# Mapping the memory's keys in the projections' layout, turning them by transposing transfers, and making a segment's sums in the next segment's query stage

## The chip, the cores and the metric

The kernel runs on one core of one Trainium2 chip. The metric is the device time of one execution in microseconds (us). A core has a matrix engine (TensorE, PE in the profile; PEld is its weight load), a vector engine (VectorE, DVE), a scalar engine (ScalarE, ACT), a general engine (GpSimd, POOL) and a queue engine that issues nearly all transfers here (SyncE, SP). Each engine works through its own instructions in the order in which they were written, and waits on semaphores for the others.

## The reference

Two independent results stand side by side in the output: an attention with a compressive memory on `A_x`, and a Fourier mixing layer on `B_x`. The change touches only the memory of the first. With 2048 rows, width 576, 32 heads of 18, cut into four segments of 512 rows:

```python
phi = lambda t: jnp.where(t > 0, t + 1.0, jnp.exp(t))
for s in range(N):
    qs, ks, vs = q[:, :, s], k[:, :, s], v[:, :, s]
    logits = jnp.einsum("bhqd,bhkd->bhqk", qs, ks) * scale + mask
    p = _softmax(logits, axis=-1)
    a_dot = jnp.einsum("bhqk,bhkd->bhqd", p, vs)
    pq = phi(qs)
    num = jnp.einsum("bhld,bhde->bhle", pq, M)
    den = jnp.einsum("bhld,bhd->bhl", pq, z)[..., None] + 1e-6
    o = g * (num / den) + (1.0 - g) * a_dot
    outs.append(o)
    pk = phi(ks)
    M = M + jnp.einsum("bhld,bhle->bhde", pk, vs)
    z = z + jnp.einsum("bhld->bhd", pk)
```

The sums M and z of a segment contract over its 512 rows, so the matrix engine needs the mapped keys `pk` with rows on the partitions.

## The kernel before

**Stages.** The first stage (to about 215 us) makes, for each of the four segments, the query and key projections and then the value projection, looks into the memory, and sums the mapped keys times the values into the memory. Float32 numbers are cut into a high and a low float16 part throughout, so a product is three matrix products. Beside this, the first stage loads and cuts the Fourier input and weights. The second stage (the rest, over three quarters of the time) interleaves the softmax attention of 32 head groups with the dense products of the Fourier layer; its order is set by a table of places and a head start of `LOW["head"]` dense steps.

**A segment in the first stage.** `open_qk(s)` writes products for the first four of nine column blocks m (0 to 3 queries, 4 to 7 keys, 8 the last 64 columns of both): first the terms of input parts k = 0 and 1 for all four blocks, then the rest. Then, for m in (0, 1, 2, 3, 8, 4, 5, 6, 7), `project_qk` makes the remaining products, ACT copies each block out (a key block stays as a float32 tile `KF[m]`, columns on the partitions, rows along it), DVE takes its largest value, POOL makes a scale from that, and for s > 0 a query block is mapped by `phi` for the memory. Then, for four row tiles j, `project_v` makes two half products of 288 columns each, ACT and DVE cut them (tiles `vs`, `vn`, `vr`), and the generator `lookup` reads the memory for s > 0.

**Mapped keys before.** In `project_v`, after the first half of tile j, `k_natural(j)` turns the five key blocks' 128 rows with five float32 PE transposes into two PSUM tiles `kt`; ACT makes relu from each (320 and 256 columns) and exp over all 576, DVE adds them (line 482, twice), casts to float16 (line 483, `knh`), and POOL or DVE subtracts for the low part (line 484, `knl`). This is done for 12 tiles: three segments of four. `kn` and `vn` have two buffers, by j. `accumulate(j)` (line 664) multiplies mapped keys with `vn[j]` into three PSUM tiles in 11 products; it stands after `project_v(j + 1)`, and that of the last tile, j = 3, inside the next segment's `open_qk`. `memory()` then reads the sums out (ACT line 673, DVE line 675), masks them on POOL, and cuts them four ticks later.

**The order.** Cuts of keys, queries, Fourier input and hidden weights are placed by the table `TIMES` in slots (13 a segment: nine projections, four row tiles); `timed(n)` writes all that is due by slot n. `ENGINES` says for each low part whether DVE (0) or POOL (1) makes it. `later(1, ...)` puts a call, mostly a transfer, into the next tick. The cut tiles `p` (two float16 parts of 512) share five buffers; each is held until its transfers have landed.

Of the kernel before, what the change touches and what calls it, by code (L numbers as in the profile page):

```python
# [12 lines left out]
F32 = mybir.dt.float32  # L13
# [11 lines left out]
P = 128  # L25
# [205 lines left out]
def infini_attention_and_fnet(ctx: ExitStack, tc: tile.TileContext, xT, wqk, w8, wv, wo, beta, xbT, cT, hT, out):  # L231
# [270 lines left out]
    def open_qk(s):  # L502
# [5 lines left out]
        for a, b in zip(edges, edges[1:]):  # L508
            for m in ms:
                for n in range(a, b):  # L510
                    pe.matmul(FIRST[m], *terms[m][n], start=n == 0, stop=n == 13)  # L511
# [88 lines left out]
    def k_natural(j):  # L600
        js = slice(j * P, (j + 1) * P)
        e = sk.tile([P, D], F32, name="ke", bufs=2)
        sources = []
        for ms in ((8, 4, 5), (6, 7)):
            o = ps.tile([P, L], F32, name="kt", tag="acc", bufs=5)
            for n, m in enumerate(ms):
                pe.transpose(o[:, n * P:(n + 1) * P], KF[m][:, js], ident)
            sources.append((e[:, :320], o[:, 64:384]) if ms[0] == 8 else (e[:, 320:], o[:, :256]))
        phi("keys", e, sources, *kn[j % 2])

    def project_v(s, j, meanwhile):
# [4 lines left out]
        for h in range(2):  # L616
# [10 lines left out]
            if s < 3:  # L627
                cut16(vn[j % 2][:, 0, hs, :DH], vn[j % 2][:, 1, hs, :DH], o)
            dve.tensor_tensor(r[:, hs], o, vs[:, hs, 18:36], OP.subtract)
            if h == 0 and s < 3:  # L630
                k_natural(j)
# [17 lines left out]
    def accumulate(j, which=(0, 1)):  # L649
        (kh, kl), v = kn[j % 2], vn[j % 2]  # L650
        for n in which:
            for c in range(5):
                b, at, both = SUMS[c]
                o = sums(c)
                fs = slice(64 + c * P, 64 + (c + 1) * P) if c < 4 else slice(0, 64)
# [7 lines left out]
                for keys, values, to in todo:  # L663
                    pe.matmul(to, keys[:, fs], values, start=b not in started, stop=True, skip_group_check=True)
                    started.add(b)
# [169 lines left out]
    def value_load(G):  # L835
        if G < NG:
# [6 lines left out]
            2.64, 2.86, 6.22, 7.98, 10.74, 10.75, 14.61, 15.81, 19.93, 18.76, 22.19, 22.72, 25.41, 26.05, 28.15,  # L843
            29.07, 33.85, 32.47, 38.83, 42.49],
        "fourier_high": [
            3.24, 5.15, 9.1, 9.18, 12.67, 12.17, 17.74, 17.24, 21.8, 19.26, 24.11, 24.59, 27.01, 27.83, 30.08, 30.44,
            35.63, 35.31, 41.59, 43.21],
        "fourier_low": [
            5.87, 7.07, 9.69, 9.65, 12.88, 15.09, 18.71, 18.31, 21.84, 20.05, 24.3, 25.26, 27.11, 28.68, 31.96, 31.13,
            37.93, 35.46, 41.63, 43.55],  # L850
        "key_high": [
            8.87, 11.85, 12.5, 11.11, 5.49, 19.93, 19.02, 22.3, 26.42, 21.45, 34.62, 35.55, 42.28, 37.46, 32.06,
            45.61, 46.36, 50.73, 48.45, 43.61],
        "key_low": [
            11.93, 12.19, 14.6, 11.93, 6.4, 19.97, 26.66, 23.27, 29.12, 21.93, 35.99, 38.96, 45.01, 38.19, 33.18,
            46.24, 47.23, 51.28, 51.81, 44.15],
        "query_high": [
            7.81, 6.66, 12.61, 11.74, 19.01, 25.83, 25.22, 25.79, 34.42, 38.56, 38.99, 36.6, 46.88, 47.84, 49.98, 48.0],
        "query_low": [
            10.08, 9.16, 13.03, 11.77, 19.53, 25.89, 25.95, 26.64, 34.54, 38.66, 39.13, 38.71, 49.92, 47.94, 50.19,  # L860
            48.47],
        "x_load": [
            8.68, 8.9, 9.11, 9.96, 10.88, 14.1, 16.66, 16.93, 18.62, 21.07, 29.06, 29.2, 32.1, 34.28, 36.66],
        "x_split": [
            11.44, 11.98, 18.79, 21.04, 34.56, 36.26],
        "hidden_high": [
            44.5, 44.99, 45.26, 46.07, 47.52],
        "hidden_low": [
            45.92, 45.29, 45.66, 50.24, 50.14]}
# [850 lines left out]
```

## Time and profile before

| | us |
|---|---|
| median of 3 runs | 932.0 (930.23 to 934.66) |
| the profiled execution | 932.74 |
| its span on the core | 931.2 |
| end of the first stage's last product on PE | about 215.5 |

PE was busy for 905.1 us of the span, DVE 743.0, ACT 694.9, POOL 560.1. These shares are means over two unlike stages. In the profile, a row of the view of groups gives line, engine, operation, tile written and tiles read, shapes, the count, busy time and mean length of one, and the idle time just before them with its releaser. A row of the view of waits says who waited for whom: us in total, how often, the longest. A row of the table of stretches gives, for a stretch of time, the busy us of PE, PEld, DVE, ACT and POOL with their instruction counts, then the granted PE clock as a share of full speed, the share of the transfer engines, and GB/s. The change lies wholly in the first stage, so its waits and stretches are what is to be read.

### The profile page before, as it was taken

How to read it: one execution, taken by the hardware profiler on the slowest of the kernel's cores; microseconds unless marked ns; L12 is line 12 of the kernel's file. 1: busy time of each engine (PE TensorE's matmuls, PEld its weight loads, DVE VectorE, ACT ScalarE, POOL GpSimd, SP SyncE). 2: the span in 40 equal slices, each digit the busy share in tenths (PEclk: the TensorE clock that was granted, in tenths of full speed). 3: DMA queues.
4: the chain of work that ended last, by engine and by line, in shares of the span. 5: the costliest groups of instructions: out<-in, count | busy, mean ns of one | idle time of the engine just before them, and what ended most of it. 6: DMA issues, size and time to landing. Idle time of an engine off the chain costs nothing.

```text
span 931.2 us, 25620 instructions
## 1 busy us (share of the span) xinstructions
PE 905.1 (97%) x9250; PEld 658.6 (71%) x9250; DVE 743.0 (80%) x2125; ACT 694.9 (75%) x1687; POOL 560.1 (60%) x843
## 2 busy tenths in 40 slices
PE   9999999998999999999999999999999999999997
PEld 5644746566677777777777777777777677777996
DVE  7878989978967768887788878887888888785784
ACT  6676768774767778888778877888789777885442
POOL 2334546544444557756786677668656896677560
PEclk9999999999999999999999999999999999999999
DMA  8466565769665437876888788887988897975552
GB/s 254 145 221 200 185 219 190 248 207 298 172 138 144 126 97 188 190 207 190 205 203 216 183 192 213 197 211 184 215 216 217 184 217 188 211 171 155 164 175 93
DMA packets 283128, 177.67 MB, mean 191 GB/s; under 512 B 204881, under 2 KB 240977, under 8 KB 282961
## 3 DMA queue, kind: packets, MB, share of 16 engines
q1 hardware_dynamic: 282768, 175.82, 70.9%
q8 instruction: 74, 1.21, 0.6%
q14 instruction: 62, 0.50, 0.2%
q10 hardware_dynamic: 224, 0.14, 0.1%
HBM read 90.00 MB, written 44.83 MB: 145 GB/s over the span
## 4 chain that ended last, share of the span: by engine, by line
PE 61%; ACT 12%; DVE 11%; DMA 5%; POOL 4%; issue 4%; SPq 1%; ACTq 0%; DVEq 0%; POOLq 0%
PE d L965 29%; PE pv L1497 4%; PE d L1009 3%; PE d L1011 3%; PE d L1010 3%; PE s L1365 3%; PE t L1251 3%; PE v L281 2%; PE pv L1498 2%; DVE s L1373 2%; ACT pd L1461 2%; PE s L1251 2%; PE d L1251 2%; ACT pf L1399 1%; PE d L1016 1%
## 5 line engine op out<-in xcount | busy, mean ns | idle before, releaser
L965 PEld LDWEIGHTS <-cs 128*128 128x128 f16 x3072 | 293.3, 98 | 84.8 <-issue 13.6
L965 PE MATMUL d<-wide,cs 128*128 128x288 f16 x2592 | 337.2, 286 | 0.0
L1373 DVE CUSTOM_DVE_ANT_0 s<-s,causal 128x384 f32<-128x384 f32 (+2 forms) x320 | 147.4, 498 | 62.6 <-PE s L1365 22.3
L1477 POOL TENSOR_TENSOR plo<-pd,phi 128x384 f16<-128x384 f32 (+1 forms) x116 | 120.0, 1054 | 3.3 <-ACT phi L1470 3.2
L1399 ACT ACTIVATE pf<-s,nb 128x384 f32<-128x384 f32 (+3 forms) x256 | 117.4, 526 | 5.0 <-DVE negm L1373 1.8
L329 POOL TENSOR_TENSOR cs<-craw,cs 128x512 f16<-128x512 f32 x88 | 103.5, 1178 | 28.9 <-ACT cs L795 26.4
L1412 POOL TENSOR_TENSOR hl<-pf,hl 128x512 f16<-128x512 f32 x50 | 58.5, 1176 | 98.4 <-ACT hl L1407 87.2
L1412 DVE TENSOR_TENSOR hl<-pf,hl 128x512 f16<-128x512 f32 (+1 forms) x142 | 94.4, 689 | 12.9 <-ACT hl L1407 12.5
L1373 DVE CUSTOM_DVE_ANT_0 t<-t,causal 128x384 f32<-128x384 f32 (+1 forms) x192 | 98.5, 541 | 2.2
L1407 ACT ACTIVATE hl<-pf 128x512 f16<-128x512 f32 (+1 forms) x192 | 93.2, 553 | 2.4 <-DMA ptt<-hl 2.4
L795 ACT ACTIVATE cs<-craw 128x512 f16<-128x512 f32 x128 | 80.4, 628 | 3.4 <-PE d L965 3.4
L1465 POOL TENSOR_SCALAR_AFFINE_SELECT pd<-pd 128x512 f32<-128x512 f32 x64 | 45.2, 706 | 61.0 <-ACT pd L1461 61.0
L1395 ACT ACTIVATE nb<-nb 128x2 f32<-128x2 f32 (+1 forms) x96 | 19.8, 206 | 72.8 <-DVE nb L1373 72.7
L1457 ACT ACTIVATE phi<-t 128x384 f16<-128x384 f32 x128 | 63.7, 497 | 6.7 <-PE t L1450 3.5
L965 PE MATMUL d<-ab,cs 128*128 128x288 f16 x480 | 66.6, 288 | 0.0
L281 PE MATMUL v<-wide,xh 128*128 128x288 f16 x256 | 49.5, 291 | 1.4 <-DVE w L717 0.6
L1365 PEld LDWEIGHTS <-st 54*128 54x128 f16 x512 | 19.6, 94 | 41.0 <-issue 35.1
L1365 PE MATMUL s<-st 54*128 54x256 f16 (+3 forms) x320 | 43.0, 296 | 5.4 <-ACT pf L1399 3.0
L511 PE MATMUL qk<-xh,wide 128*128 128x512 f16 x128 | 43.0, 391 | 0.6 <-ACT xh L251 0.4
L511 PEld LDWEIGHTS <-wide 128*128 128x128 f16 x224 | 21.4, 100 | 28.8 <-issue 4.9
L1019 ACT ACTIVATE wide<-d 128x288 f16<-128x288 f32 x54 | 22.2, 416 | 24.7 <-PE d L1016 24.1
L281 PE MATMUL qk<-xh,wide 128*128 128x512 f16 x128 | 40.7, 379 | 0.0
(346 smaller groups left out, 2319.6 us busy)
## 6 DMA issues: line engine op xcount, KB each, us to landing
craw<-cT SPq DMA_DIRECT2D x128, 256.0 KB
vd<-vs SPq DMA_DIRECT2D x16, 440.0 KB
vst<-vd SPq DMA_DIRECT2D x32, 220.0 KB
st<-qd SPq DMA_DIRECT2D x64, 108.0 KB
st<-kd SPq DMA_DIRECT2D x64, 108.0 KB
wide<-xbT SPq DMA_DIRECT2D x20, 256.0 KB
xk<-xd SPq DMA_DIRECT2D x20, 256.0 KB
out<-y SPq DMA_DIRECT2D x16, 288.0 KB
```

Of the source, the lines that this page charges most:

```text
L281: pe.matmul(o, a, b, start=n == 0, stop=n == len(terms) - 1)
L329: fn(*a)
L511: pe.matmul(FIRST[m], *terms[m][n], start=n == 0, stop=n == 13)
L795: act.activation(t[:, 0], raw, AF.Copy)
L965: pe.matmul(o[h], a, b[:, h * 288:h * 288 + 288], start=start, stop=stop)
L1251: pe.matmul(o, a, b, start=first and i == 0, stop=True, skip_group_check=True)
L1365: pe.matmul(o[half][:, first + c:first + c + w], q[r, x, i * P:w], k[r, x, :w], start=True, stop=True)
L1373: dve.tensor_tensor_reduce(x, x, CAUSAL[0][:, L - w:], scale=scale, scalar=-LOWEST, op0=OP.add, op1=OP.min, accum_out=into[:, 4 * half + i ...
L1399: act.activation(f[kind][half][:, to:to + w], o[half][:, c:c + w], AF.Exp, bias=nb[:, 4 * half + i:4 * half + i + 1], scale=-1.0)
L1407: act.activation(hl[half][:, 0, F_COL[kind]:F_COL[kind + 1]], f[kind][half], AF.Copy)
L1412: engine.tensor_tensor(hl[half][:, 1, a:b], f[kind][half], hl[half][:, 0, a:b], OP.subtract)
L1477: engine.tensor_tensor(lo[:, a:b], f, hi[:, a:b], OP.subtract)
```

## The change

Each key block is mapped where it lies, columns on the partitions, by the new `key_features(n)`: relu from `KF`, exp, one DVE add and one DVE cast over 512 rows, and the low part. There are 15 of these, three segments of five blocks; the last block of a segment has 64 partitions and a tile of its own, `k8`, the other four take a `p` tile. One transposing transfer per block then writes both parts, eight squares of 128 by 128, into `kn[c]`. The 60 PE transposes and their `kt` tiles go. `vn` gets four buffers, `kn` one for each block. All four `accumulate` calls of a segment move to the next segment's query stage: two behind the second projection and two behind the third, with `memory()` behind them. `TIMES` gets a row for the 15 features and new numbers elsewhere, `ENGINES` new choices, `LOW["head"]` goes from 3 to 2.

```diff
-    kn = []
+    kn = [sk.tile([P, 8, P], F16, name=f"kn{c}") for c in range(5)]
+    k8 = sk.tile([P, 2, L], F16, name="k8")
+    pool.memset(k8[:64], 0.0)
...
-    for i in range(2):
-        kn.append(tuple(sk.tile([P, D], F16, name=f"kn{n}{i}") for n in "hl"))
+    for i in range(4):
...
-                if s and m == 0 and a:
-                    accumulate(3, (1,))
-            if s and a == 0:
-                accumulate(3, (0,))
...
-    def k_natural(j):
-        js = slice(j * P, (j + 1) * P)
-        e = sk.tile([P, D], F32, name="ke", bufs=2)
-        sources = []
-        for ms in ((8, 4, 5), (6, 7)):
-            o = ps.tile([P, L], F32, name="kt", tag="acc", bufs=5)
-            for n, m in enumerate(ms):
-                pe.transpose(o[:, n * P:(n + 1) * P], KF[m][:, js], ident)
-            sources.append((e[:, :320], o[:, 64:384]) if ms[0] == 8 else (e[:, 320:], o[:, :256]))
-        phi("keys", e, sources, *kn[j % 2])
+    def key_features(n):
+        s, c = divmod(n, 5)
+        rows = slice(0, P) if c < 4 else slice(64, P)
+        e = sk.tile([P, L], F32, name="ke", bufs=2)[rows]
+        t = sb.tile([P, 2, L], F16, name="p", tag="p", bufs=5) if c < 4 else k8
+        phi("keys", e, ((e, KF[c + 4][rows]),), t[rows, 0], t[rows, 1])
+        later(1, nc.sync.dma_start_transpose, kn[c], t.rearrange("p a t -> p (a t)"))
...
-            if h == 0 and s < 3:
-                k_natural(j)
...
-        (kh, kl), v = kn[j % 2], vn[j % 2]
+        v = vn[j]
...
-                fs = slice(64 + c * P, 64 + (c + 1) * P) if c < 4 else slice(0, 64)
+                kh, kl = (kn[c][:, j + i, 64 * (c // 4):] for i in (0, 4))
...
         "x_split": [
-            11.44, 11.98, 18.79, 21.04, 34.56, 36.26],
+            10.72, 10.49, 18.71, 17.16, 35.42, 34.9],
...
+        "keys": [
+            11.53, 7.47, 10.5, 12.1, 6.81, 22.03, 20.47, 24.9, 24.5, 20.2, 33.58, 34.3, 36.16, 37.5, 33.77]}
...
-        "query": [0, 0, 0, 1, 0, 0, 1, 0, 0, 0, 1, 1, 1, 0, 0, 1],
-        "queries": [0, 1, 1, 0, 0, 1, 1, 1, 0, 1, 0, 1, 1, 0, 0],
-        "keys": [1, 1, 1, 0, 1, 1, 1, 1, 1, 1, 1, 1],
-        "value": [0, 1, 1, 0, 1, 1, 1, 1, 1, 1, 1, 1, 1, 0, 1, 0],
-        "look": [1, 1, 0, 0, 0, 1, 0, 0, 0, 1, 1, 1],
-        "hidden": [0, 1, 1, 0, 0, 1]}
+        "query": [0, 0, 1, 1, 1, 1, 1, 0, 0, 0, 1, 1, 1, 1, 1, 0],
+        "queries": [0, 1, 0, 1, 0, 1, 1, 1, 0, 1, 1, 1, 1, 0, 1],
+        "keys": [0, 1, 1, 1, 0, 0, 0, 1, 0, 1, 0, 0, 1, 0, 1],
+        "value": [0, 1, 1, 0, 0, 1, 1, 1, 1, 0, 1, 1, 1, 0, 1, 1],
+        "look": [1, 1, 0, 0, 0, 0, 0, 0, 0, 0, 0, 0],
+        "hidden": [1, 0, 0, 0, 0, 1]}
...
+    AGENDA.extend((t, key_features, n) for n, t in enumerate(TIMES["keys"]))
...
-        if s:
-            memory()
-        else:
+        if s == 0:
             tick()
...
+            if s and 0 < n < 3:
+                for j in (2 * n - 2, 2 * n - 1):
+                    accumulate(j)
+            if s and n == 2:
+                memory()
...
-            if more and j:
-                accumulate(j - 1)
```

Three places show what stands where. The first is PE at the start of segment 1. In the kernel before, the last products of the sums of row tile 2 (`m`, from the low keys `knl`) run straight into the opening query products:

```order
L664 MATMUL m_267<-vn_251,knl_250 128x152
L664 LDWEIGHTS knl_250
L664 MATMUL m_268<-vn_251,knl_250 64x76
L511 LDWEIGHTS wide [waits DVE_49,PE_49]
L511 MATMUL qk<-xh_137,wide 128x512 [waits Activation_49]
L511 LDWEIGHTS wide
L511 MATMUL qk<-xl_139,wide 128x512 [waits DVE_49]
```

In the changed kernel the opening products follow the last value product directly, and the sums begin where the 56 opening products end:

```order
L512 LDWEIGHTS wide
L512 MATMUL qk<-xt,wide 128x512
L656 LDWEIGHTS kn_249 [waits DMAHW2_49]
L656 MATMUL m_276<-vn_256,kn_249 128x304 [waits Pool_49]
L656 LDWEIGHTS kn_250 [waits DMAHW6_49]
L656 MATMUL m_277<-vn_256,kn_250 128x304
L656 LDWEIGHTS kn_251 [waits DMAHW6_49]
L656 MATMUL m_278<-vn_256,kn_251 128x304
L656 LDWEIGHTS kn_252 [waits DMAHW6_49]
L656 MATMUL m_276<-vn_256,kn_252 128x152
```

What moved: the sums of a segment stand behind the next segment's opening, and their first products wait for the transposing transfers (the waits on DMAHW) of all of the segment's blocks.

The second place is DVE late in segment 0, before and after the first value tile. Before, the sequence is a Fourier low part (`p` from `wide`), a key block's largest value, and then the value cut with the mapped keys from `kt`:

```order
L437 SCALAR_TENSOR_TENSOR p<-wide,p 128x512 [waits DMAHW3_49]
L520 TENSOR_REDUCE mx<-kf 128x1 [waits Activation_49]
L253 TENSOR_TENSOR vn_251<-v,vn_251 128x16x18 [waits PE_49,Activation_49]
L629 TENSOR_TENSOR vr<-v,vs_259 128x288
L482 SCALAR_TENSOR_TENSOR ke<-kt,ke 128x320 [waits PE_49,Activation_49]
L482 SCALAR_TENSOR_TENSOR ke<-kt,ke 128x256 [waits PE_49]
L483 CAST knh_249<-ke 128x576 [waits DVE_49]
```

In the changed kernel the mapping stands among the key blocks, one block at a time, read from `kf`:

```order
L483 SCALAR_TENSOR_TENSOR ke<-kf,ke 64x512 [waits Activation_49]
L484 CAST k_254<-ke 64x512 [waits DVE_49]
L485 TENSOR_TENSOR k_254<-ke,k_254 64x512 [waits DVE_49]
L517 TENSOR_REDUCE mx<-kf 128x1 [waits Activation_49]
L437 SCALAR_TENSOR_TENSOR p<-wide,p 128x512 [waits DMAHW3_49]
L483 SCALAR_TENSOR_TENSOR ke<-kf,ke 128x512 [waits Activation_49]
L484 CAST p<-ke 128x512 [waits DVE_49]
```

What moved: the mapping no longer waits for PE, but now takes three DVE instructions for many of the blocks, and its cast is the first to write a `p` tile.

The third place is SP in segment 0, where the input of segment 1 (`xT`) is loaded. Before, behind the stores of the last key block:

```order
L554 DMA kd_69<-p 64x512
L426 DMA wide<-xbT 128x512 [waits DMAHW3_49,DVE_49]
L329 DMA xd_81<-p 128x1024 [waits DMAHW4_49]
L340 DMA raw<-xT 128x512 [waits DMAHW5_49]
L340 DMA raw<-xT 128x512 [waits DMAHW6_49]
L329 DMA vd_73<-vs_259 128x1760 [waits DMAHW7_49,DVE_49,Pool_49]
```

In the changed kernel:

```order
L551 DMA kd_69<-p 64x512
L329 DMA_TRANSPOSE kn_253<-k_254 128x8x128 [waits DMAHW3_49,DVE_49,Pool_49]
L426 DMA wide<-xbT 128x512 [waits DMAHW4_49,DVE_49]
L329 DMA xd_81<-p 128x1024 [waits DMAHW5_49]
L329 DMA_TRANSPOSE kn_250<-p 128x8x128 [waits DMAHW6_49,Pool_49]
L340 DMA raw<-xT 128x512 [waits DMAHW7_49]
L340 DMA raw<-xT 128x512 [waits DMAHW0_49]
```

What moved: two transposing transfers, each waiting for a low part on DVE or POOL, stand ahead of the loads of segment 1's input.

More of the change, by code (lines that the diff above doesn't have):

```diff
@@ L663, in accumulate @@
                 for keys, values, to in todo:
-                    pe.matmul(to, keys[:, fs], values, start=b not in started, stop=True, skip_group_check=True)
+                    pe.matmul(to, keys, values, start=b not in started, stop=True, skip_group_check=True)
                     started.add(b)
@@ L848, in infini_attention_and_fnet @@
+            30.48, 35.67, 35.06, 41.55, 43.17],
         "fourier_low": [
-            5.87, 7.07, 9.69, 9.65, 12.88, 15.09, 18.71, 18.31, 21.84, 20.05, 24.3, 25.26, 27.11, 28.68, 31.96, 31.13,
-            37.93, 35.46, 41.63, 43.55],
+            5.87, 7.07, 9.69, 9.65, 12.88, 15.09, 18.71, 18.53, 21.07, 20.05, 24.4, 25.51, 27.12, 28.69, 31.96, 31.17,
+            37.97, 35.21, 41.59, 43.51],
         "key_high": [
-            8.87, 11.85, 12.5, 11.11, 5.49, 19.93, 19.02, 22.3, 26.42, 21.45, 34.62, 35.55, 42.28, 37.46, 32.06,
@@ L853, in infini_attention_and_fnet @@
-            45.61, 46.36, 50.73, 48.45, 43.61],
+            8.0, 11.85, 12.5, 16.02, 5.63, 19.06, 23.96, 22.3, 26.42, 21.83, 33.92, 35.55, 42.5, 37.46, 32.2, 45.61,
+            46.36, 50.29, 48.28, 44.73],
         "key_low": [
-            11.93, 12.19, 14.6, 11.93, 6.4, 19.97, 26.66, 23.27, 29.12, 21.93, 35.99, 38.96, 45.01, 38.19, 33.18,
-            46.24, 47.23, 51.28, 51.81, 44.15],
+            11.93, 12.19, 14.6, 16.84, 6.54, 19.1, 31.6, 23.27, 29.12, 22.45, 35.12, 38.96, 45.23, 38.19, 34.57,
```

22 lines of the change are left out of this document (11 added, 11 removed).

## The prediction

> **What bounds the kernel now.** I read the stretches of the first stage first, cut where DVE ends a segment, since the change lies in that stage alone.
>
> ```profile
> 5.00:57.50 52.50, 50.41 (x303) 28.93 (x301) 44.56 (x86) 39.01 (x85) 14.65 (x31) 0.99 0.73 225
> 57.50:118.00 60.50, 57.83 (x361) 34.13 (x360) 50.98 (x117) 44.96 (x101) 28.53 (x45) 0.95 0.53 178
> 118.00:171.00 53.00, 51.57 (x347) 31.74 (x346) 47.40 (x110) 40.54 (x95) 28.87 (x45) 1.00 0.60 204
> 171.00:222.00 51.00, 46.25 (x305) 27.92 (x303) 43.11 (x93) 34.52 (x76) 31.97 (x53) 0.99 0.79 259
> ```
>
> The first busy number is PE, the third DVE. PE looks full, but it shares that place with DVE: in the third stretch DVE is busy for 47.4 of 53 us. To see who holds whom, I read the waits of PE, DVE and ACT up to 222 us (DVE from 5 us).
>
> ```profile
> PE kt L607 <- ACT kf L569: 2.0, 3, 1.6
> PE s L1365 <- DVE nd L708: 2.0, 1, 2.0
> PE t L1365 <- DVE w L717: 1.5, 1, 1.5
> PE qk L511 <- DVE xl L255: 1.2, 1, 1.2
> ```
>
> ```profile
> DVE qe L482 <- POOL sc L531: 4.4, 3, 1.5
> ...
> DVE xl L255 <- ACT xh L251: 3.1, 3, 1.9
> ...
> DVE mf L675 <- ACT mf L673: 2.4, 2, 1.5
> DVE ke L482 <- ACT ke L480: 1.9, 4, 0.5
> ...
> DVE ke L482 <- POOL vs L638: 0.6, 1, 0.6
> ```
>
> ```profile
> ACT vs L637 <- DVE vr L629: 14.4, 14, 2.5
> ...
> ACT p L539 <- DMA xd<-p: 1.6, 2, 1.4
> ```
>
> PE waits for DVE, and ACT waits 14.4 us for DVE, but no row has DVE waiting for PE. The stage's end says the same on PE and DVE:
>
> ```profile
> 215.24 0.23 PE L705 MATMUL look<-md,pq_hi 128*128 128x152 f16 x1
> ```
>
> ```profile
> 220.11 0.19 DVE L717 TENSOR_TENSOR w<-look,g 128x32 f32<-128x32 f32 x1
> ```
>
> PE finishes the last lookup product at 215.5, DVE its last `w` at 220.3, and the two waits of `s` and `t` above are PE standing for just that. So the stage ends with DVE; an instruction taken from PE pays only where DVE then comes sooner. Behind the stage PE is the bound of a long, unchanged program, so I let a microsecond of the stage's end count as one of the total.
>
> **What PE loses.** Twelve times five transposes. Their pace is the step from their start to the next product's:
>
> ```profile
> 38.97 0.71 PE L607 MATMUL kt<-ident,kf 128*128 128x128 f32 x5
> 39.52 0.41 PE L281 MATMUL v<-wide,xh 128*128 128x288 f16 x2
> ```
>
> That is 0.55 us for five, 12 x 0.55 = 6.6 us, and the 2.0 us that `kt` waited for ACT: 8.6 us. The sums stay 132 products; they only change place. By the reading above I count none of the 8.6 us by itself.
>
> **What DVE gets.** The groups of DVE, shapes kept apart, from the start to 232 us:
>
> ```profile
> L482 DVE SCALAR_TENSOR_TENSOR ke<-kt,ke 128x320 f32<-128x320 f32 x12 | 5.8, 484 | 2.5 <-ACT ke L480 1.9 <-POOL vs L638 0.6
> L483 DVE CAST knh<-ke 128x576 f16<-128x576 f32 x12 | 5.7, 476 | 0.4
> L482 DVE SCALAR_TENSOR_TENSOR ke<-kt,ke 128x256 f32<-128x256 f32 x12 | 4.9, 412 | 0.0
> ...
> L484 DVE TENSOR_TENSOR knl<-ke,knh 128x576 f16<-128x576 f32 x1 | 0.8, 759 | 0.0
> ```
>
> Removed: 12 x (0.484 + 0.412 + 0.476) + 0.759 = 17.2 us. Nothing in the trace adds a relu to a float32 block that lies in SBUF as `kf`; the nearest rows are the same operation for the queries, and a cut that reads `kf`:
>
> ```profile
> L545 DVE SCALAR_TENSOR_TENSOR p<-kf,sc,p 128x512 f16<-128x512 f32 x15 | 11.2, 749 | 2.6 <-ACT p L539 2.6
> ...
> L482 DVE SCALAR_TENSOR_TENSOR qe<-qk,qe 128x512 f32<-128x512 f32 x12 | 8.2, 684 | 1.4 <-ACT qe L480 1.4
> ...
> L545 DVE SCALAR_TENSOR_TENSOR p<-q,sc,p 128x512 f16<-128x512 f32 x10 | 8.0, 804 | 0.7 <-ACT p L539 0.7
> L719 DVE TENSOR_TENSOR am<-nd,w 128x576 f32<-128x576 f32 x6 | 6.2, 1029 | 0.2
> ...
> L483 DVE CAST pq_hi<-qe 128x512 f16<-128x512 f32 x12 | 5.6, 468 | 0.4
> ...
> L484 DVE TENSOR_TENSOR pq_lo<-qe,pq_hi 128x512 f16<-128x512 f32 x5 | 3.5, 693 | 0.2
> ...
> L638 DVE TENSOR_TENSOR vs<-vr,vs 128x576 bf16<-128x576 f32 x4 | 3.1, 770 | 0.8 <-ACT vs L637 0.8
> ...
> L484 DVE TENSOR_TENSOR pq_hi<-qe,pq_hi 64x512 f16<-64x512 f32 x2 | 1.4, 685 | 0.1
> ...
> L483 DVE CAST pq_hi<-qe 64x512 f16<-64x512 f32 x3 | 1.3, 420 | 0.1
> ...
> L747 DVE TENSOR_TENSOR wide<-raw,wide 128x576 f16<-128x576 f32 x1 | 0.7, 747 | 0.0
> ```
>
> Between 0.684 and 0.749 I take 0.684, the same operation; the other end adds 1.0 us. Added: 15 x 0.684 = 10.3; casts 12 x 0.468 + 3 x 0.420 = 6.9; of the low parts eight fall to DVE, 5 x 0.693 + 3 x 0.685 = 5.5. Together 22.7, so the mapping costs DVE 22.7 - 17.2 = **5.5 us more**. The table of engines moves other low parts: four more `am` to DVE (+4.1), four query cuts away (-4 x 0.804 = -3.2), two query lows away (-1.4), one `vs` and one hidden weight more (+0.8 and +0.7): **+1.0**. DVE gets 6.5 us.
>
> Against it stand the waits of DVE tied to what goes. The 2.4 of `mf` go: the sums are then read behind three query blocks. The mapping's 1.9 + 0.6 go, since relu and exp now come from a block copied out long before. The 1.9 of `xl` at the start of segment 1 goes if the earlier split finds its input loaded. That is 6.8, so DVE's net is 6.5 - 6.8 = **-0.3 us**. With no wait gone it is +6.5; with all of the DVE rows shown gone (12.4) it is -5.9.
>
> **What is hidden.** ACT's 36 mapping instructions become 30, and four query cuts that go to POOL bring one more copy each; with 40.5 of 53 us busy and 14.4 spent waiting for DVE I count it at nothing, and up to 1 us if DVE stops being behind. POOL has four such operations fewer in all and holds no row of the end. SP issues 15 transposing transfers. The nearest row has 20 squares, 640 KB, instead of 8:
>
> ```profile
> 246.33 2.57 SPq L1416 DMA_TRANSPOSE ptt<-hl  x1
> ```
>
> ```profile
> 246.30:251.00 4.70, 4.70 (x41) 3.36 (x39) 4.24 (x15) 2.96 (x9) 0.00 (x0) 1.00 0.70 158
> ```
>
> So 2.57 x 8 / 20, about 1.0 us of SP each (the bounds are near nothing and 2.57), and in the 4.7 us from issue 158 GB/s x 4.7 us = 743 KB moved, enough for that whole transfer: 8 squares should land some 3 us after issue. The cover is the opening of the next segment, 56 products:
>
> ```profile
> 20.73 0.38 PE L281 MATMUL qk<-xh,wide 128*128 128x512 f16 x1
> 20.95 0.38 PE L281 MATMUL qk<-xl,wide 128*128 128x512 f16 x1
> ```
>
> 56 x 0.22 = 12.3 us. Only block 3 of segment 0 is issued so late (slot 12.1, one tick on) that this cover could fail; a miss costs PE 1 to 2 us once, and most of it falls while DVE is behind anyway. Nothing for it. One page speaks against this part: the Trainium skill, "VectorE: DVE Perf Modes", section "The three transpose paths", gives 390 ns for a 128x128 bf16 square through TensorE and 1309 ns through the transfer engines, and its rules name TensorE first where PSUM will do. By that figure of the Trainium skill, square after square, an estimate of 8 x 1.309 = 10.5 us per block would leave under 2 us of the cover, and a block that waits behind another would be late; the trace, with 20 squares through within 4.7 us, speaks against it.
>
> Behind a waiting transposing transfer on SP stand the loads of segment 1's input: two issues of 1.0 us and a low part on POOL ahead of them, while the split is asked for one slot sooner. If ACT stands there, the 1.9 us credit is lost and one or two more with it.
>
> **The rivals.**
> - *PE decides after all* (0.22). If DVE's lag is only the shadow of PE's order, the 8.6 us come through: 932.7 - 8.6 = **924.1**. For it: PE is busy for 57.8 of 60.5 us in the second stretch. Against it: no wait of DVE names PE.
> - *The p tiles* (0.18), the slower side. The cast on DVE is now the first writer of 12 `p` tiles and waits until an earlier store has landed; 56 uses of five buffers become 68. ACT paid that twice, 1.6 us. Six casts at 0.8 us make 4.8: 932.4 + 4.8 = **937.2**. From about five on, the kernel is measurably slower, because DVE holds the end.
> - *Input late behind the transposes* (0.07): 1.9 lost and 1 more: **935.3**.
> - *Transposed keys late* (0.05): 15 transfers share engines that are busy at 0.53 to 0.79. If each segment's first sums stand 1 us longer than DVE's lag hides, it is 932.4 + 3 x 1 = **935.4**. This is where the slow square of the Trainium skill ("VectorE: DVE Perf Modes", "The three transpose paths") would lead; the two rows above make it unlikely.
> - *Nothing arrives* (0.08): the turn to the second stage is held by its loads, which keep a transfer share of 0.79 over the last stretch. **932.7**.
>
> **How the numbers follow.** The sum is made against the profiled execution, 932.7 (its span is 931.2, with 1.5 around it), which is 0.7 above the median of the runs: 932.7 - 0.3 = 932.4, or 931.7 against the median; I say **932.0**, between the two. My forecast, DVE holding the end with its gain and loss near balance, has 0.40. Low end: rival one, 924. High end: 932.7 + 6.5, no wait gone, 939. Half a per cent, 4.7 us, is about what a measurement can tell from no change. Faster by more: rival one and 0.03 of the forecast's tail, 0.25. Slower by more: 0.15 of the p tiles and 0.05 from the tails of the forecast and of the two late transfers, 0.20. The rest, 0.55, is within.
>
> **What would show it.** In the changed profile DVE's last `w` of the stage should lie at 218 to 223 us, DVE's busy time up to there some 6 us higher, and PE should wait for DVE by several us more in the first stage than now. If PE's waits don't grow and `w` comes by 213, rival one is right. A row of DVE's casts waiting for stores of `p` shows the second; ACT's `xh` of segment 1 waiting for `xT` the third. I am wrong in the mechanism if the sums wait for `kn` in every segment, or if the second stage, unchanged in work, takes another time.

## The result, and the profile after

The changed kernel takes 942.0 us (median of four runs, 939.4 to 944.5) beside 931.5 (930.2 to 934.7) for the kernel before on the same chip: a ratio of 1.0101, interval 1.0083 to 1.0118 (the two medians lie 1.1% apart). It is 1% slower, and lies above the forecast's range.

The profiled execution of the changed kernel took 944.5 us, the slowest of its four. I cut the first stage where PE turns from one kind of work to the other: value stage of segment 0, then query and value stage of segments 1, 2 and 3. The table of stretches, cut so, of the kernel before (stretch, length, then busy us of PE, PEld, DVE, ACT and POOL, granted clock, transfer share, GB/s):

```profile
32.80:53.20 20.40, 20.16 (x167) 15.74 (x165) 15.87 (x32) 15.28 (x35) 9.11 (x16) 1.00 0.74 209
53.20:85.70 32.50, 30.73 (x139) 13.49 (x139) 27.96 (x53) 23.30 (x50) 11.13 (x23) 0.95 0.57 196
85.70:114.10 28.40, 25.73 (x214) 19.63 (x212) 23.63 (x63) 22.06 (x56) 15.22 (x21) 0.94 0.63 212
114.10:142.70 28.60, 28.60 (x139) 13.26 (x139) 24.52 (x47) 20.15 (x42) 14.87 (x25) 1.00 0.53 181
142.70:168.00 25.30, 23.87 (x214) 18.88 (x212) 23.77 (x65) 21.30 (x54) 14.29 (x23) 1.00 0.65 222
168.00:196.60 28.60, 28.60 (x139) 13.20 (x139) 25.59 (x49) 21.27 (x44) 14.89 (x28) 1.00 0.66 219
196.60:215.50 18.90, 17.63 (x163) 14.42 (x162) 15.13 (x42) 15.06 (x35) 12.59 (x22) 1.00 0.83 264
sum 182.70, PE 175.33 PEld 108.62 DVE 156.47 ACT 138.42 POOL 92.10; mean PE 25.05 PEld 15.52 DVE 22.35 ACT 19.77 POOL 13.16
```

And of the changed kernel:

```profile
33.00:51.30 18.30, 14.73 (x114) 11.16 (x113) 14.17 (x25) 11.74 (x25) 5.53 (x12) 0.93 0.89 207
51.30:90.40 39.10, 36.28 (x171) 16.34 (x171) 32.12 (x59) 28.32 (x60) 17.11 (x29) 0.90 0.73 214
90.40:114.70 24.30, 19.54 (x162) 14.77 (x161) 21.30 (x54) 18.02 (x42) 12.59 (x17) 0.93 0.78 231
114.70:151.30 36.60, 33.01 (x173) 15.69 (x171) 30.03 (x58) 26.97 (x57) 19.57 (x32) 1.00 0.67 204
151.30:174.80 23.50, 18.25 (x162) 13.98 (x161) 22.31 (x58) 16.36 (x40) 8.22 (x12) 1.00 0.73 209
174.80:211.30 36.50, 34.31 (x172) 16.04 (x171) 28.50 (x55) 24.42 (x53) 20.96 (x33) 0.95 0.61 202
211.30:231.50 20.20, 17.79 (x163) 14.43 (x162) 16.54 (x42) 15.67 (x36) 13.93 (x21) 1.00 0.87 289
sum 198.50, PE 173.92 PEld 102.41 DVE 164.97 ACT 141.48 POOL 97.91; mean PE 24.85 PEld 14.63 DVE 23.57 ACT 20.21 POOL 13.99
```

Each query stage grew by 6.6 to 8.0 us, and the value stages gave back 2.1, 4.1 and 1.8 us (the last one grew). Before, two query stages were full for PE: 28.60 of 28.60 us. Over the stretch PE is busy about as long (175.3 and 173.9 us), although 60 transposes have gone, 6.2 us in a run below; its granted clock there fell from 0.98 to 0.96. It now stands idle for 24.6 us in place of 7.4, and DVE has 8.5 us more work.

The stage ends 16 us later on PE, the execution 11.8 us later (944.5 against 932.7), because the span has 711.2 us behind the stage in place of 715.7. That is a part of the change, and not an answer to the late start: in the profiled executions of the runs below (those of 6,400 us left out) it is 713.6 to 717.8 us in every run built on the kernel before and 709.9 to 711.7 us in every run built on the changed one, however late the stage ends. The number `LOW["head"]`, 2 in place of 3, may be the reason; no run changes it alone.

The waits of PE in the changed kernel, up to 240 us:

```profile
PE look L689 <- DVE vr L623: 11.2, 7, 2.2
PE qk L512 <- DVE vr L623: 6.3, 3, 2.8
PE v L281 <- DVE vr L623: 2.7, 2, 2.4
```

`vr` is DVE's last read of a value product, which frees its PSUM tile: in the value stages and at the openings PE now stands for DVE. Before, these were the rows:

```profile
PE look L703 <- DVE vr L629: 1.2, 2, 0.8
...
PE look L697 <- DVE vr L629: 1.0, 1, 1.0
```

No row of the changed kernel's PE names `kn`. The waits of DVE and of ACT in the same stretch:

```profile
DVE qe L483 <- ACT qe L481: 8.0, 11, 1.4
...
DVE ke L483 <- ACT ke L481: 3.7, 2, 3.2
DVE mf L667 <- ACT mf L665: 2.8, 3, 2.1
...
DVE xl L255 <- ACT xh L251: 2.1, 2, 1.6
```

```profile
ACT vs L629 <- DVE vr L623: 21.2, 13, 3.4
ACT mf L665 <- PE m L656: 8.2, 3, 3.5
...
ACT q L566 <- PE qk L512: 5.8, 2, 3.4
```

Of the waits that the prediction let go, those of `mf` (2.4 us before) and of the mapping, `ke` (2.5 before), are still there and somewhat longer. The 1.9 us of `xl` at the start of segment 1 did go; what is left of `xl` lies at 8 and 10 us, in the first split. The waits of `qe` grew from 5.8 us (4.4 put down to POOL's scales, 1.4 to ACT) to 8.0, all put down to ACT.

### The profile page after: what moved, and what is told of

Read it like the earlier page. It is cut to its first block, busy times and chain, and to the rows that moved or that the text cites. A ratio compares the mean times of both kernels' runs of the same rounds, so it can differ in the third digit from the quotient of the medians.

```text
span 942.7 us, 25497 instructions
## 1 busy us (share of the span) xinstructions
PE 902.0 (96%) x9190; PEld 651.2 (69%) x9190; DVE 752.0 (80%) x2126; ACT 698.9 (74%) x1685; POOL 562.9 (60%) x844
## 4 chain that ended last, share of the span: by engine, by line
PE 57%; ACT 11%; DVE 10%; POOL 4%; issue 4%; DMA 2%; SPq 0%; DVEq 0%; ACTq 0%; POOLq 0%
PE d L961 27%; PE pv L1493 4%; PE d L1005 3%; PE d L1006 3%; PE d L1007 3%; PE s L1361 3%; PE t L1247 2%; DVE s L1369 2%; PE pv L1494 2%; ACT pd L1457 2%; PE s L1247 2%; PE d L1247 2%; ACT hl L1403 2%; ACT pf L1395 1%; PE d L1012 1%
## 5 line engine op out<-in xcount | busy, mean ns | idle before, releaser
L512 PEld LDWEIGHTS <-wide 128*128 128x128 f16 x224 | 22.4, 103 | 42.2 <-issue 10.9
L1361 PEld LDWEIGHTS <-st 54*128 54x128 f16 x512 | 19.7, 94 | 39.4 <-issue 31.9
L281 PEld LDWEIGHTS <-wide 128*128 128x128 f16 x224 | 22.0, 98 | 26.4
```

The costliest lines, as they stand in the source:

```text
L281: pe.matmul(o, a, b, start=n == 0, stop=n == len(terms) - 1)
L1361: pe.matmul(o[half][:, first + c:first + c + w], q[r, x, i * P:w], k[r, x, :w], start=True, stop=True)
```

## The experiments

All ratios are against the kernel before, run on the same chip. Where I compare ends of the first stage, I mean the end of PE's last lookup product in one profiled execution each: 215.5 us before, 231.5 us in the changed kernel.

**The sums moved alone.** The kernel before, with its transposes, but four buffers for `kn` and `vn` and the sums and the readout placed as in the change.

```diff
+            if s and 0 < n < 3:
+                for j in (2 * n - 2, 2 * n - 1):
+                    accumulate(j)
+            if s and n == 2:
+                memory()
...
-            if more and j:
-                accumulate(j - 1)
```

> The kernel before with one part of the change: the key transposes on TensorE and their mapping stay, but kn and vn get four buffers and all sums of a segment stand behind the next segment's second and third projection, with the memory's readout behind them. Theory S (sums): in the changed kernel's trace the query stage of segments 2 and 3 is 36.6 us on PE against 28.5 before, the value stage only 2 us shorter; PE is the bound of the query stage and DVE of the value stage, so the three row tiles' sums (3 x 1.23 us a segment) were moved from where PE stood to where PE is needed: slower than the kernel before by 4 to 11 us, 936 to 943. Theory P (the p buffers): nothing here takes a p buffer, 931 to 933. Theory D (the added DVE work): DVE does what it did, 931 to 933.

945.95 us, 1.0129 (1.0108 to 1.0150): 11.6 us slower. The move that the prediction costed at nothing costs by itself as much as the whole change. (The first stage ends at 227.7 us, 12.2 later than before, beside 16.0 later in the changed kernel.)

**More `p` buffers.** The changed kernel with `bufs=8` for `p`.

> The changed kernel with eight p buffers in place of five. Theory P: ACT's 7.5 us of standing for stores and transposing transfers of p (1.8 before) go, and the waits of DVE for ACT behind them: 6 to 8 us faster than the changed kernel, 934 to 936. Theory S: at most 1 to 2 us, since the order of PE's work is what holds, 940 to 942. Theory D: 940 to 942.

941.23 us, 1.0077 (1.0056 to 1.0098), against 1.0101 for the change: some 2 us by the ratios, 3.7 by the medians, and the intervals overlap. ACT's waits for `p` tiles are gone from its rows, though its waits for loads of `wide` rose from 2.9 to 5.3 us. This rival was small at most.

**The keys' low halves on POOL.** The changed kernel with fifteen ones in `ENGINES["keys"]`.

> The changed kernel with all 15 low parts of the mapped keys on POOL, eight of which were on DVE (5.5 us of DVE work). Theory D: DVE holds the end of the stage, so 4 to 6 us faster than the changed kernel, 936 to 938. Theories S and P: within 2 us of it, 940 to 943; worse if the transposing transfers then wait for POOL.

943.48 us, 1.0108 (1.0085 to 1.0131): nothing gained.

**The sums put back.** The changed kernel with eight `p` buffers, the keys mapped at slots 6.8 to 9.5, the sums of tile 0 behind the third value tile, of tiles 1 and 2 behind the fourth, of tile 3 in the next opening, and the readout behind it.

> The changed kernel with eight p buffers, the key blocks mapped right behind their projections (slots 6.8 to 9.5 of a segment), and the sums placed as before: tile 0 behind the third value tile, 1 and 2 behind the fourth, 3 inside the next opening, with the memory's readout there. Theory S: the 3.7 us a segment leave the query stage, so 5 to 10 us faster than the run with eight buffers alone. Theory P: as the run with eight buffers alone, 934 to 936. Theory D: the same as it too; DVE gets the mapping earlier, and the value stage later pays for it.

953.11 us, 1.0196 (1.0172 to 1.0220). The query stages went back to 28.5 us each, but in the value stages PE now waits for the transposed keys:

```profile
PE m L660 <- DMA kn<-p: 10.3, 4, 5.1
```

At these places the sums in the value stage come too early for keys that come by transfer. The earlier mapping is mixed into this run; the run with the keys mapped earlier, below, has it without the moved sums.

**More products, by place.** The kernel before with 33 sum products more per segment, on values of zero, so that the sums stay what they are: once in the openings, once in the value stages.

```diff
             if s and a == 0:
+                for j in (2, 2, 2):
+                    accumulate(j, v=vz)
                 accumulate(3, (0,))
```

> The kernel before, with 33 more products in each of the three openings after the first (eleven sums' products three times, with values of zero, so the sums stay what they are); nothing else moves. Theory S (PE holds the end of the query stage, so a product there costs its time): 33 products of 0.11 us are 3.7 us in each of three stages, 11 us at the end of the first stage, about 10 us in all after the second stage gives a little back: 941 to 946 us where before has 932 to 934. Rival W (what costs in the change is the waiting around the sums: the late readout of the memory, the opening's banks): PE has room for the products, 0 to 3 us.

944.29 us, 1.0116 (1.0099 to 1.0133): 10.4 us of the 11.

```diff
                 accumulate(j - 1)
+                accumulate(j - 1, v=vz)
```

> The kernel before, with the same 33 products of zero values, but in the value stages (each of the three sums there a second time). Theory S: PE waits for DVE in the value stage, so they cost little: 0 to 3 us, 932 to 937 us. Rival A (PE's products cost the same anywhere in the first stage): 33 times 0.11 us in three segments, 11 us, as in the run with the zero products in the openings.

941.09 us, 1.0076 (1.0059 to 1.0093): 7.2 us. So PE's products cost nearly their time in the query stages. In the value stages they cost it too: these grew by 3.5, 4.3 and 4.1 us, and some 4 us came back in the query stage of segment 1, which lasts 28.5 us in place of 32.5. Theory S was right on the first and wrong on the second.

**The readout late.** The kernel before with only `memory()` moved behind the third projection.

> The kernel before with the sums where they were, but the memory read out and masked behind the third projection as in the change. Theory S: nothing, within 2 us of before, since neither PE nor DVE gets more work. Rival W (the late readout costs: ACT's and DVE's part of it falls among the query features, and the lookups wait for it): 4 us or more slower.

938.87 us, 1.0054 (1.0037 to 1.0070): 5.0 us for work that is neither more nor less. The waits of ACT:

```profile
ACT q L569 <- PE qk L511: 10.6, 5, 3.9
...
ACT mf L673 <- DVE mf L675: 4.9, 3, 2.2
```

Three projections later the readout stands among the query features. Yet the query stages last as long as before (32.5, 28.5 and 28.9 us), and the value stages behind them grow by 0.8, 1.9 and 1.4 us; behind the stage PE stands 2.2 us for the transfer of a lookup's result (`amd`), a wait that the kernel before does not show. That the lookups get the memory late is the likely way; no row here shows it.

**Sums early, by feature tile.** The changed kernel with eight `p` buffers; of each segment, the tiles whose keys were expected to have landed by then are summed in the value stage.

> The changed kernel with eight p buffers, its sums split by feature tile: those whose transposed keys have landed by then (two, three and four of five tiles in the three segments) are summed for token tiles 0 to 2 in the same segment's value stage, behind the third and the fourth value tile; the rest stays behind the second and third projection. That takes 6, 9 and 12 of 20 parts of the sums out of the query stages: 4.9 us times 27 over 20 are 6.6 us. Theory S: 4 to 7 us faster than the changed kernel with eight buffers (941), so 934 to 937 us. Rival A (PE's products cost the same anywhere): 941 us, no change. Rival K (PE waits for the transposed keys, as with all the sums put back): slower than 941.

944.98 us, 1.0123 (1.0104 to 1.0142): slower than with eight buffers alone. Its waits of PE show rival K:

```profile
PE m L656 <- DMA kn<-p: 7.3, 3, 5.4
PE m L656 <- DVE vn L253: 2.0, 3, 1.3
```

**The transposes left out.** The kernel before, `k_natural` reading `KF` as it stands, so the memory is that of untransposed keys; DVE's and ACT's instructions keep their widths, but read the keys from SBUF.

```diff
-            o = ps.tile([P, L], F32, name="kt", tag="acc", bufs=5)
-            for n, m in enumerate(ms):
-                pe.transpose(o[:, n * P:(n + 1) * P], KF[m][:, js], ident)
+            o = KF[ms[j % 2]]
```

> The kernel before without its 60 transposes: the keys' map reads the keys as they stand (untransposed, so the sums and the lookups get other values), with the same instructions on ACT and DVE and the same sums at the same places. It gives what the loss of the transposes is worth by itself. PE is busy 98.8, 90.6 and 94.3% of the three value stages, and loses 2.2 us of transposes in each and 2.0 us of waits for ACT's copies of the keys. Theory S (PE holds every stage, another chain lies close behind it in the value stages): PE's 8.6 us come out in part, 3 to 7 us faster than before, 927 to 931 us. Rival D (DVE holds the value stages, as the prediction had it): within 1 us of before.

933.11 us beside 933.08, 1.0002 (0.9986 to 1.0017). The row of the whole stretch:

```profile
32.40:215.20 182.80, 169.16 (x1104) 101.96 (x1103) 158.13 (x347) 138.05 (x310) 92.00 (x153) 0.98 0.64 212
```

PE lost 6.2 us of work (175.3 to 169.2), and the stretch lasts 182.8 us in place of 182.7. More work on PE costs, less gains nothing that shows: another chain lies about as far out. The relief is not quite pure. Three of the twelve pairs of adds (`ke`) took 1.6 to 2.1 us in place of 0.8, each beside a POOL operation, and DVE's work in the stretch grew by 1.7 us, so a gain of about that size may be hidden; 6.2 us are not.

**DVE loaded alone.** The kernel before with all twelve low halves of the keys on DVE, eleven of them from POOL.

> The kernel before with all 12 low halves of the mapped keys on DVE: 11 of them come from POOL, 11 times 0.76 us are 8.3 us more for DVE in the first stage, and PE as it was. If DVE holds the first stage, as the prediction had it: 5 to 8 us slower, 938 to 942 us. If PE alone holds it and DVE's 26 us of idle time there are room: within 2 us of before.

940.16 us, 1.0073 (1.0053 to 1.0093): 6.7 us of the 8.3. That is the other chain:

```profile
32.70:222.40 189.70, 178.82 (x1164) 109.13 (x1163) 163.07 (x358) 137.99 (x310) 77.80 (x143) 0.96 0.62 204
```

DVE's work grew by 6.6 us in the stretch (156.5 to 163.1), the stretch by 7.0, and DVE's idle time stayed at 26 to 27 us. So that idle time was no slack; the rows of DVE's waits name ACT and POOL.

**One token tile summed.** The changed kernel, and then the run with the sums moved alone, each with the sums of the fourth token tile only; the first three are left out of the memory.

```diff
-                for j in (2 * n - 2, 2 * n - 1):
-                    accumulate(j)
+                if n == 2:
+                    accumulate(3)
```

> The changed kernel with the sums of the fourth token tile alone (the first three are left out, so the memory gets other values); their place, the mapping, the transfers and the late readout stay. Theory S: 33 products fewer in each of three query stages that PE holds, 3.7 us each, about 10 us: 930 to 934 us. Rival W (the waits around the sums cost, the products nothing): 939 to 942 us.

941.07 us, 1.0089 (1.0072 to 1.0106): the 33 products fewer per segment gain 1 us by the ratios, 2.6 by the medians, and the intervals overlap. (The stage ended at 225.7 in its profiled execution, 5.8 us sooner than in that of the change; but the one was the fastest of its four at 937.8 us, the other the slowest of its own, so the medians decide.) The stages show where the products' time went: the query stages last 35.0, 33.7 and 31.9 us in place of 39.1, 36.6 and 36.5, and the value stages of segments 1 and 2 last 26.5 and 27.1 in place of 24.3 and 23.5. Most of what PE gains in the one it waits for in the other. Theory S falls for the changed kernel.

> The kernel before with the sums moved alone, and of them only the fourth token tile's made (33 products fewer in each of three query stages; the memory gets other values). Theory S (PE's products in the query stage cost there): 946 less 8 to 11, 935 to 938 us. Theory W (the place and the late readout cost, not the products): 943 to 946 us.

938.53 us, 1.0057 (1.0040 to 1.0073). With the transposes and the old mapping in place, the same edit gains 0.7% (from 1.0129), some 7 us, and what is left, 5.1 us, is about what the late readout cost alone. So the sums' move is taken apart: about 7 us of products, 5 us of readout. In the changed kernel the products are for the most part hidden behind something else.

**Keys mapped earlier.** The changed kernel with eight `p` buffers and the mapping at slots 6.8 to 9.5, the sums where the change put them.

> The changed kernel with eight p buffers and the keys mapped in the second half of the query stage (at slots 6.8 to 9.5 of 13) in place of 6.8 to 12.1; the sums stay in the next query stage. Theory B (in the value stages the mapping on ACT and DVE stands ahead of the work that frees the banks of v, and PE waits for it): value stages 1 to 3 us shorter each, query stages as they are, 932 to 938 us. Rival N (that work is only moved ahead of other work for the same banks): 940 to 943 us.

942.85 us, 1.0111 (1.0093 to 1.0129): no gain, rival N.

**The mapping left out.** The changed kernel without the fifteen maps and transfers, `kn` all zeros; then this with one token tile's sums. With such a memory the kernel's own test of its denominators sends it, behind the fast program, through a slow exact one, so these runs last 6,400 us; of them I use the end of the first stage and differences among themselves.

> The changed kernel without its 15 maps of keys and their transfers (the transposed keys are zeros, so the memory gets other values); all 44 sums per segment and the late readout stay. Theory T (PE and the chain of ACT and DVE hold it side by side, both about 10 us later than before): PE still holds the query stages with their 44 products, 938 to 942 us. Theory D (ACT and DVE alone hold it): the maps are 15 times some 1.6 us of DVE and 1.15 us of ACT, 17 to 24 us, so 930 us or less. Theory R (the late readout holds it): 937 us or more.

> The changed kernel without the maps and with the sums of the fourth token tile alone (the memory gets other values). Theory T: both are relieved, PE by 11 us and ACT and DVE by over 17, so 925 to 932 us, while either alone stays at 938 or more. Theory R: 5 us above that, 935 us or more.

6,413.4 and 6,405.5 us. Their stretches:

```profile
37.40:212.80 175.40, 166.03 (x1105) 100.60 (x1104) 142.08 (x307) 123.20 (x275) 84.52 (x144) 1.00 0.68 224
```

```profile
34.60:205.20 170.60, 156.21 (x1006) 93.72 (x1005) 141.48 (x307) 122.33 (x275) 85.19 (x144) 0.99 0.70 230
```

Without the mapping the stage ends at 212.8 in place of 231.5, though every sum is still made: theory D's 12 us or more came. Theory T is half right. The query stages still last 34.2 to 34.9 us, of which PE is busy for 33.0: there PE holds them. The value stages fall from 18.3, 24.3 and 23.5 us to 13.7, 17.8 and 18.7, and PE's waits for `vr` fall with them:

```profile
PE look L691 <- DVE vr L625: 3.8, 5, 1.8
...
PE qk L514 <- DVE vr L625: 1.7, 3, 0.8
```

So what the mapping costs in the changed kernel is to a large part that DVE comes late to the reads that free the value products. And with the mapping gone, PE's products count again: 4.8 us by the stretches, 7.6 at the stage's end (2.8 of them lie ahead of the first value stage, where no sums are made), 7.9 in the total.

**One tile, readout early.** The changed kernel with the fourth tile's sums of two or three feature tiles, made in the opening, and the readout at its old place; the rest is left out.

> The changed kernel with the sums of the fourth token tile alone, and of it the two or three feature tiles whose keys have landed by then, made in the opening as before the change, with the memory's readout right behind the opening (the rest of the sums is left out; the memory gets other values). Against the run with one tile's sums and the late readout (941): theory R: 4 to 6 us faster, 935 to 937 us. Theory T (ACT and DVE hold it there): 939 to 942 us.

Its memory has zeros too (6,425.7 us). The stage ends at 227.5, no sooner than with the readout late (225.7): in the changed kernel the readout's place is hidden as well, as far as one profiled execution each can tell. DVE's busy time differs between the two, 169.1 and 163.8 us, so the comparison is rough.

**Both reliefs together.** The changed kernel with one token tile summed and all key lows on POOL.

> The changed kernel with the sums of the fourth token tile alone and all 15 low halves of the mapped keys on POOL: the two edits that gained nothing alone, together (three token tiles' sums are left out, so the memory gets other values). Theory T (PE's sums and DVE's mapping hold it side by side): now both are relieved, 933 to 937 us. Theory N (a third thing holds it, such as the way ACT, DVE and POOL wait for each other): 939 to 943 us.

940.82 us, 1.0078 (1.0058 to 1.0097): theory N, by its number. The stretch, and that of one tile summed alone ahead of it:

```profile
33.20:225.70 192.50, 159.81 (x1006) 94.13 (x1005) 163.75 (x346) 140.11 (x305) 97.52 (x151) 0.97 0.73 224
```

```profile
33.30:228.30 195.00, 164.03 (x1006) 95.72 (x1005) 161.88 (x338) 140.49 (x306) 106.23 (x159) 0.95 0.74 222
```

Eight subtractions of 0.69 us went from DVE, but its work fell by only 1.9 us (by 2.0 in the run with the key lows on POOL alone) and its idle time rose from 28.8 to 33.1, so DVE was hardly relieved and the test of theory T is weak. In the run with the key lows on POOL alone, two of the twelve wide adds of a mapped key took 1.4 and 1.7 us and one cast 1.26, each beside a POOL operation, where the others took 0.69 and 0.43; DVE waited 6.6 us for ACT's `ke` in place of 3.7 there and here; and here DVE's cast stood 2.4 us for `p` tiles whose transfers had not ended, in place of 0.8. Both reliefs with more `p` buffers were not tried.

**A version faster than both.** The kernel before with eight `p` buffers.

> The kernel before with eight p buffers in place of five. ACT waits 1.8 us for p buffers there. PE holds the stages and does not wait for what ACT would do earlier: within 1 us of before by theory S. If the buffers are worth what they were in the changed kernel: 2 to 3 us faster.

931.76 us beside 933.08, 0.9985 (0.9975 to 0.9995): a small gain that can be measured, and the only version here that is faster.

## Why the prediction was wrong

**The step that failed first:** "The sums stay 132 products; they only change place." A change of place has a price. Before, two of the three query stages were full for PE, and the products brought there cost about 7 us; the readout that follows them cost 5 us by standing later. Alone, that is 11.6 us where the sum had nothing. The view that shows it was at hand: the prediction cut the stretches where DVE ends a segment, which mixes both stages, and read 47.4 of 53 us. Cut where PE changes its work, the same trace reads 28.60 of 28.60.

**The second step that failed:** DVE's ledger, "6.5 - 6.8 = -0.3 us". The work side was mis-sized, the wait side wrong. DVE's busy time up to its last `w`, before and after:

```profile
5.00:220.30 215.30, 204.51 (x1305) 121.86 (x1302) 184.35 (x402) 159.04 (x353) 102.44 (x172) 0.98 0.65 214
```

```profile
5.00:236.50 231.50, 204.86 (x1257) 116.82 (x1257) 194.28 (x406) 163.63 (x352) 106.61 (x176) 0.96 0.73 220
```

It rose by 9.9 us, not 6.5. The groups of DVE in the changed kernel:

```profile
L483 DVE SCALAR_TENSOR_TENSOR ke<-kf,ke 128x512 f32<-128x512 f32 x12 | 9.2, 766 | 3.7 <-ACT ke L481 3.7
...
L484 DVE CAST pq_hi<-qe 128x512 f16<-128x512 f32 x12 | 6.6, 546 | 0.4
L484 DVE CAST p<-ke 128x512 f16<-128x512 f32 x12 | 5.1, 427 | 0.6
...
L485 DVE TENSOR_TENSOR p<-ke,p 128x512 f16<-128x512 f32 x5 | 3.5, 692 | 0.2
...
L485 DVE TENSOR_TENSOR k<-ke,k 64x512 f16<-64x512 f32 x3 | 2.1, 689 | 0.1
L483 DVE SCALAR_TENSOR_TENSOR ke<-kf,ke 64x512 f32<-64x512 f32 x3 | 2.1, 688 | 0.1
...
L484 DVE CAST k<-ke 64x512 f16<-64x512 f32 x3 | 1.3, 424 | 0.1
```

The mapping's six rows come to 23.3 us where 22.7 were forecast, so most of the missing 3.4 us lies in instructions that the change does not touch, such as the casts of the queries (0.468 to 0.546 us). These are means, and single long instructions make them. The view of the tile `ke` gives the shortest, the middle and the longest add in ns, and the timeline what ran beside the longest:

```profile
L483 DVE SCALAR_TENSOR_TENSOR ke<-kf,ke x15: 676/685/1655, 34.3 to 175.8; 128x512 f32<-128x512 f32 x12, 64x512 f32<-64x512 f32 x3
```

```profile
102.04 1.54 POOL L711 TENSOR_TENSOR am<-nd,w 128x576 f32<-128x576 f32 x1 [2.67 <-DVE w L709]
102.47 1.66 DVE L483 SCALAR_TENSOR_TENSOR ke<-kf,ke 128x512 f32<-128x512 f32 x1
```

So the prediction's 0.684 was right for the add itself; what its ledger had no term for is an instruction that is stretched beside one of POOL. And of the 6.8 us of waits only the 1.9 of `xl` went: the idle time of DVE in that stretch rose from 31.0 us to 37.2. A wait on an engine in a chain of three is not a sum that can be struck out; the run with DVE loaded alone shows DVE's 26 us of idle staying put when its work grows.

**A smaller step:** "Behind the stage PE is the bound of a long, unchanged program, so I let a microsecond of the stage's end count as one of the total." The second stage took 4.5 us less in the changed kernel, which is one of the prediction's own signs that its mechanism is wrong. By that much the execution hides what the first stage lost.

**Right, as far as it went:** "So the stage ends with DVE", and that the 8.6 us of the transposes count for nothing: leaving them out gains nothing that shows. But it was half of the matter, since PE lay about as far out; the rival that PE decides was as true of added work as it was false of removed work. PE did come to wait for DVE by several us more, as the prediction's sign had it. The transposed keys came in time everywhere in the changed kernel, as forecast, though only because the sums stand so late: earlier sums waited for them. No row of ACT waits for the input of segment 1 either. The issue of a block took 1.23 us or more on SP where 1.0 was the estimate.

**The `p` tiles** gave the rival on the slower side. In the changed kernel they held up ACT, not DVE's cast, and were worth 2 to 4 us with overlapping intervals, beside the 4.8 of the prediction.

**How the parts add up.** They don't. The sums' move alone is 11.6 us; the new mapping with hardly any sums in the query stage, though with the late readout, is 8 us; together they are 10.6 us. By the ends of the first stage, which leave the shorter second stage out, they are 12.2, 10.2 and 16.0 us in one profiled execution each. In the changed kernel the mapping's chain covers most of what the sums cost. What exactly holds that chain stays open. Moving DVE's subtractions to POOL, moving the mapping's slots or taking away PE's products gained nothing clear of the error, but the first of these relieved DVE by 2 us only. That it is the mapping as a whole, its work on ACT, DVE and POOL with its transfers, is shown by leaving it out; how these share it is not. The new tables of places and engines were not run without the mapping's change; in the run without the mapping they are in force and the stage ends no later than before, though the old mapping's work is gone there too. Moving adds and casts to another engine was not tried.

## What to carry to other kernels

Before work is moved between stages, cut the profile at the stage boundaries of the engine that gets it: an average of 95% can be a full stage beside one with room, and work that keeps its amount can cost by its new place. In a kernel that is tuned to balance, two engines can lie about equally far out: here relief of PE alone was worth nothing that shows, and more load on PE or on DVE cost most of its time. Price both sides by a run each, one that adds and one that takes away. A wait inside a chain of in-order engines is not a credit: here one of three went, and the idle time grew. Look at the longest instruction of a group beside its mean.

## What the runs showed of the hardware

The transposing transfer of a block, eight 128 by 128 squares, holds SP's queue for 1.23 us or somewhat more (up to 1.66). The timeline of SP in the changed kernel (start, length, line, what it issues):

```profile
95.46 1.23 SPq L329 DMA_TRANSPOSE kn<-k  x1
97.34 1.23 SPq L329 DMA_TRANSPOSE kn<-p  x1
...
106.35 1.23 SPq L329 DMA_TRANSPOSE kn<-p  x1
```

That is some 0.15 us per square, beside 0.13 for the transfers of twenty squares in the second stage. The last block of segment 0 is issued at 66.88 us, and PE multiplies with it, without a wait, from the fourth of the sums' products on, which begin at 69.94. So its eight squares landed within some 3.5 us of the issue, near the 3 us of the prediction and far from its 10.5 us for square after square.

DVE's instructions with both sources in SBUF were at times stretched beside a POOL operation: eleven of the twelve wide adds of a mapped key took about 0.69 us in the changed kernel, the one beside `am` on POOL took 1.66. The same holds for casts from SBUF, 1.34 us for one of the queries in place of 0.43, beside `p` on POOL. The adds that read one source from PSUM were not stretched: in the kernel before the mapping's 24 took 0.41 to 0.49 us each, and with the keys read from SBUF in their place (the run without transposes) the longest took 1.47. That reading the keys from SBUF is what lays the adds open to POOL is what these rows suggest; only that one run changes it, and it drops the transposes too.
